# A gated attention unit with a hypermixer: a quarter of each diagonal block turned instead of scored, and transposes by four row tiles

## The chip, the cores and the metric

The kernel runs on one core of a Trainium2 chip. A core has five engines, each with its own instruction stream: TensorE (PE in the profile, with its weight loads PEld beside it), VectorE (DVE), ScalarE (ACT), GpSimd (POOL) and SyncE (SP), which here only issues DMAs. The metric is device time in microseconds, as the median of several runs; less is better. The profile is of one execution, so a span in it stands a little apart from the median of the runs.

## The reference

Eight batches of S = 3200 rows; `u` and `v` have 256 columns, `z` has 64, and the hidden width of the second part is 64.

```python
def _attn_ref(u, v, z):
    scale = 1.0 / S
    scores = scale * np.matmul(z, z.transpose(0, 2, 1))
    attn = np.maximum(scores, 0.0) ** 2
    out = np.matmul(attn, v)
    return (u * out).astype(np.float32)

def _moe_ref(x, w_q, w_k, w_out):
    wq = x @ w_q
    wk = x @ w_k
    scale = 1.0 / np.sqrt(d_hyper)
    W_tok = scale * np.einsum('bsd,btd->bst', wq, wk)
    mixed = np.einsum('bst,btd->bsd', W_tok, x)
    return (np.maximum(mixed, 0.0) @ w_out).astype(np.float32)

def reference(u, v, z, moe_w_q, moe_w_k, moe_w_out):
    return _moe_ref(_attn_ref(u, v, z), moe_w_q, moe_w_k, moe_w_out)
```

`scores` is symmetric, and so is `attn`: a block above the diagonal is the transpose of the one below it.

## The kernel before

The 3200 rows of a batch are 25 row tiles of 128. The columns of `attn` are taken in seven groups: 0 to 5 of 512 columns (four row tiles each) and group 6 (`LASTG`) of the last 128. A group's result needs every row tile's block of `attn` for the group's columns, as weights of a product with `v` that adds up in two PSUM banks.

Such a block comes in one of two ways. It is scored: `scores` multiplies z with z (line 307), `first_stage` takes relu and a scale (DVE at 321 or ACT at 319), `second_stage` squares into a 16-bit buffer `at` (POOL at 332 or ACT at 330). Or it is turned: where `is_turned` says so, the block was scored for an earlier group, and a DMA transpose (line 351, SP's queue) brings its mirror image into a `tt` buffer, or a `ts` buffer for group 6. `tiles` lists in order what is scored: (batch, group, row tile). Two entries make a pair, which shares one PSUM tile of 2 x 512 columns, because z has 64 columns and TensorE's rows hold two of them side by side. `at` has `NAT` = 11 buffers, each for one pair, and a transpose is issued per pair, with 8 blocks of 128 x 128 when both rows go to the same place.

The loop `while groups` runs in phases k. A phase scores three pairs (two when a mixing product "m" takes a place), takes their relu, squares the three pairs of the phase before, and does the second product (`second_product`, emitted at line 369) for row tiles scored at least `LAG` = 2 phases earlier, or turned (`left`). Each phase's TensorE instructions stand in a fixed order: the upper and the lower 64 rows of the array are two lanes (`Streams`, `first_pass`, `second_pass`), each of which does half of the contraction. A row tile of a wide group has four blocks, each done in two halves of 64 rows: eight matmuls 64x256. Extra products go into phases by `mix_due`, `key_due` and the table `chosen`: keys and heads "k", mixing "m", projections "p". When a group is complete, `gate` multiplies by `u` (ACT 506, DVE 507, POOL 509; for group 6 of all but the last batch ACT 499, DVE 500, POOL 501 and 502). `turn_x` and `turn_keys` issue further transposes.

The next batch's data come during the current one, at phases counted from the batch's start: `load_piece` loads pieces of v and z and casts them a few phases later (line 151, POOL on even phases, ACT on odd ones; the tables `V_FIRST` for batch 1 and `V_LATER` for the others give load phase and delay), `turn_z` transposes z, and `spread_z` copies it on ACT (184, 188), to have it in both halves of the partitions.

The order of instructions on each engine is the program's order (`manual_schedule`), and waits come from the data and the buffers. All DMAs of the loop are issued by SP in order. The diff touches the buffers, the list `tiles`, the three stages, `weights`, the tables and the choice among turned rows.

Of the kernel before, what the change touches and what calls it, by code (L numbers as in the profile page):

```python
# [9 lines left out]
FP16 = mybir.dt.float16  # L10
# [6 lines left out]
def kernel(  # L17
# [45 lines left out]
    pat = ctx.enter_context(tc.tile_pool(name="pat", bufs=NAT))  # L63
# [40 lines left out]
    zd0 = {}  # L104
# [130 lines left out]
    LASTG = NG - 1  # L235
# [18 lines left out]
    for b in range(B):  # L254
        for gi in range(NG):
            near = [t for t in range(NT) if is_turned(gi, group_of(t))]
            own = [
                t for t in range(NT) if t not in near and not is_turned(group_of(t), gi)
            ]
            if gi == LASTG:  # L260
                own = [t for t in own if group_of(t) not in FOR_SMALL]
            if b == 0 and gi == 0:
                order = [t for n0, nn in ZCH for t in range(n0, n0 + nn)]
                assert sorted(order) == sorted(near + own)
            else:
# [7 lines left out]
                for _, two in at_:  # L273
                    order = order + two
                if rest and len(rest) % 2:
                    order.remove(rest[-1])
                    order.append(rest[-1])
# [18 lines left out]
    def scores(p0, lead=0):  # L296
        pair = tiles[p0 : p0 + 2]
        sc = ps_tile("sc")
        ats = [[], []]
        for h, (b, gi, tis) in enumerate(pair):  # L300
            w = widths[gi]
            half = h * dqk
            for i in range(W // w):
                ti = tis[min(i, len(tis) - 1)]
                ats[h].append((i * w, h, w, b, ti, starts[gi], half))
        for at, h, w, b, ti, gs, half in sorted(ats[0] + ats[1], key=lambda x: (x[0], x[1] ^ lead)):
            nc.tensor.matmul(  # L307
                out=sc[:, h, at : at + w],
                lhsT=zT[b][half : half + dqk, ds(z_at(b, h) + ti * P, P)],
                rhs=zT[b][half : half + dqk, ds(z_at(b, h) + gs, w)],  # L310
                start=True,
                stop=True,
            )
        return sc

    def first_stage(p0, sc, on_act):
# [6 lines left out]
            )  # L323
        return g

    def second_stage(p0, g, on_act):
        at = pat.tile([P, 2 * W], FP16, tag="at", name="at")
        out = at[:].rearrange("p (a w) -> p a w", a=2)
        if on_act:
            nc.scalar.square(out=out, in_=g[:])  # L330
        else:
            nc.gpsimd.tensor_mul(out=out, in0=g[:], in1=g[:])  # L332
        blocks, turns = [], []
        for h, (b, gi, tis) in enumerate(tiles[p0 : p0 + 2]):
            for i, ti in enumerate(tis):
                made[b, gi, ti] = (at, h * W + i * widths[gi])
            gj = group_of(tis[0])
            if is_turned(gi, gj) or (gj == LASTG and gi in FOR_SMALL):
                blocks.append((b, gi, gj, tis[0] - starts[gj] // P, 1, h * W, (h + 1) * W))
        if len(blocks) == 2 and blocks[0][:3] == blocks[1][:3] and blocks[1][3] == blocks[0][3] + 1:  # L340
            blocks = [blocks[0][:4] + (2, blocks[0][5], blocks[1][6])]
        for b, gi, gj, n0, nn, c0, c1 in blocks:
            if gj == LASTG:
                turned[b, gi, gj] = ptt.tile([P, 1, 4, P], FP16, tag=f"ts{gi}", name=f"ts{gi}")
            elif (b, gi, gj) not in turned:
                home = tt_of[b, gi, gj]
                turned[b, gi, gj] = ptt.tile([P, 4, 4, P], FP16, tag=f"tt{home}", name=f"tt{home}")
            out = turned[b, gi, gj][:].rearrange("p n j t -> p (n j) t")
            turns.append(
                lambda out=out[:, 4 * n0 : 4 * (n0 + nn), :], c0=c0, c1=c1:  # L350
                nc.sync.dma_start_transpose(out=out, in_=at[:, c0:c1])
            )
        return turns

    accs = {}

# [509 lines left out]
    def group_begun(k, b, gi):  # L866
# [5 lines left out]
        if gi == 0 and b + 1 < B:  # L872
# [155 lines left out]
    while groups:  # L1028
# [325 lines left out]
```

## Time and profile before

| | |
|---|---|
| median of 3 runs | 765.5 us (765.41 to 766.83) |
| profiled execution, span | 763.7 us |
| TensorE busy | 754.3 us, 99% |
| weight loads | 618.0 us, 81% |
| ScalarE busy | 551.1 us, 72% |
| GpSimd busy | 537.1 us, 70% |
| VectorE busy | 461.9 us, 60% |
| DMA queue q1, share of 16 engines | 91.2% |
| mean granted TensorE clock | 0.998 |

The span is the time from the first to the last instruction of the profiled execution. In rows of the profile, a line number such as L369 stands for the program's line, `out<-in` for the buffers, and `xN` for the number of instructions in a group. "Idle before" is the time for which an engine had nothing to do ahead of such an instruction, with what released it. TensorE overlaps its matmuls, so the duration of one is longer than the step from one to the next.

### The profile page before, as it was taken

How to read it: one execution, taken by the hardware profiler on the slowest of the kernel's cores; microseconds unless marked ns; L12 is line 12 of the kernel's file. 1: busy time of each engine (PE TensorE's matmuls, PEld its weight loads, DVE VectorE, ACT ScalarE, POOL GpSimd, SP SyncE). 2: the span in 40 equal slices, each digit the busy share in tenths (PEclk: the TensorE clock that was granted, in tenths of full speed). 3: DMA queues.
4: the chain of work that ended last, by engine and by line, in shares of the span. 5: the costliest groups of instructions: out<-in, count | busy, mean ns of one | idle time of the engine just before them, and what ended most of it. 6: DMA issues, size and time to landing. Idle time of an engine off the chain costs nothing.

```text
span 763.7 us, 29059 instructions
## 1 busy us (share of the span) xinstructions
PE 754.3 (99%) x12888; PEld 618.0 (81%) x12888; DVE 461.9 (60%) x458; ACT 551.1 (72%) x651; POOL 537.1 (70%) x351
## 2 busy tenths in 40 slices
PE   9999999999999999999999999999999999999996
PEld 6777888888888887888888888888878888888884
DVE  7655676546755567555665557656566565755534
ACT  8666776677767777687776877759777697776555
POOL 7897797768766678676787668866688665854540
PEclk9999999999999999999999999999999999999999
DMA  8999789887999969997899998999899999798636
GB/s 178 189 197 219 187 187 192 174 181 160 206 196 233 219 166 185 221 235 195 214 177 219 243 195 181 158 228 265 135 223 189 228 250 156 161 222 193 176 74 262
DMA packets 289614, 150.23 MB, mean 197 GB/s; under 512 B 265168, under 2 KB 268752, under 8 KB 289488
## 3 DMA queue, kind: packets, MB, share of 16 engines
q1 hardware_dynamic: 288768, 146.48, 91.2%
q0 software_dynamic: 576, 1.64, 1.1%
q8 instruction: 100, 1.64, 0.9%
q14 instruction: 26, 0.21, 0.1%
q10 hardware_dynamic: 144, 0.26, 0.1%
HBM read 59.38 MB, written 26.21 MB: 112 GB/s over the span
## 4 chain that ended last, share of the span: by engine, by line
PE 97%; DVE 2%; issue 0%; DMA 0%; ACT 0%; DVEq 0%; ACTq 0%
PE acc L369 72%; PE sc L307 12%; PE fo L369 5%; PE qk L369 5%; PE mx L657 1%; DVE x_sb L507 1%; DVE fo L1312 0%; DVE g L321 0%; PE ztp L130 0%; DMA z<-in_z_dram 0%; PE qk L610 0%; DVE zT L136 0%; PE xtx L634 0%; PE hd L644 0%; ACT fo L1316 0%
## 5 line engine op out<-in xcount | busy, mean ns | idle before, releaser
L321 DVE TENSOR_SCALAR g<-sc 128x1024 f32<-128x1024 f32 x329 | 400.5, 1223 | 240.5 <-PE sc L307 225.9
L332 POOL TENSOR_TENSOR at<-g 128x1024 f16<-128x1024 f32 x229 | 431.4, 1893 | 131.1 <-DVE g L321 106.5
L369 PE MATMUL acc<-v_sb,at 64*128 64x256 f16 (+1 forms) x7187 | 461.8, 269 | 1.6 <-DVE x_sb L507 0.5
L369 PEld LDWEIGHTS <-at 64*128 64x128 f16 (+1 forms) x7187 | 353.9, 94 | 86.9 <-PE acc L369 25.4
L330 ACT ACTIVATE at<-g 128x1024 f16<-128x1024 f32 x227 | 236.1, 1056 | 14.3 <-DVE g L321 7.2
L369 PE MATMUL acc<-v_sb,tt 64*128 64x256 f16 x2552 | 178.7, 269 | 0.0
L307 PE MATMUL sc<-zT 64*128 64x512 f16 (+1 forms) x1008 | 165.3, 357 | 0.2
L319 ACT ACTIVATE g<-sc 128x1024 f32<-128x1024 f32 x127 | 130.0, 1024 | 45.5 <-PE sc L307 43.2
L369 PEld LDWEIGHTS <-tt 64*128 64x128 f16 x2552 | 130.1, 94 | 14.2
L509 POOL TENSOR_TENSOR x_sb<-gt,u_sb 128x512 f16<-128x512 f32 x48 | 61.2, 1276 | 66.2 <-ACT gt L506 61.8
L678 ACT ACTIVATE rt<-mx 128x1024 f16<-128x1024 f32 x47 | 47.9, 1024 | 32.6 <-PE mx L657 32.5
L506 ACT COPY gt<-acc 128x512 f32<-128x512 f32 x48 | 28.0, 584 | 46.5 <-PE acc L369 44.7
L307 PEld LDWEIGHTS <-zT 64*128 64x128 f16 x1008 | 51.9, 94 | 8.8 <-issue 1.7
L369 PE MATMUL fo<-wo,rt 64*128 64x256 f16 (+1 forms) x696 | 57.9, 270 | 0.0
L544 ACT CAST qk<-qk 128x512 f16<-128x512 f32 x47 | 27.5, 585 | 34.3 <-PE qk L369 31.6
L369 PEld LDWEIGHTS <-rt 64*128 64x128 f16 (+1 forms) x696 | 35.5, 94 | 15.3 <-PE fo L369 6.3
L507 DVE TENSOR_TENSOR x_sb<-acc,u_sb 128x512 f16<-128x512 f32 x48 | 33.2, 691 | 20.3 <-PE acc L369 19.5
L739 ACT ACTIVATE fo<-fo 128x1024 f32<-128x1024 f32 x39 | 39.9, 1024 | 1.9 <-PE fo L369 1.7
L369 PEld LDWEIGHTS <-x_sb 64*128 64x128 f16 x672 | 29.8, 95 | 4.5 <-PE qk L369 0.9
L369 PE MATMUL qk<-kx,x_sb 64*128 64x64 f16 x672 | 32.8, 190 | 0.0
L369 PE MATMUL qk<-xT_sb,wkq 64*128 64x512 f16 (+3 forms) x118 | 25.8, 326 | 0.0
L369 PE MATMUL qk<-xT_sb,wqk 64*128 64x384 f16 (+3 forms) x148 | 24.8, 296 | 0.0
(86 smaller groups left out, 275.2 us busy)
## 6 DMA issues: line engine op xcount, KB each, us to landing
u_sb<-in_u_dram SPq DMA_DIRECT2D x48, 512.0 KB, 5.5
out_dram<-fo SPq DMA_DIRECT2D x43, 512.0 KB, 4.1
piece<-in_v_dram SPq DMA_DIRECT2D x42, 512.0 KB, 5.2
piece<-in_z_dram SPq DMA_DIRECT2D x7, 512.0 KB, 5.2
tt<-at SPq DMA_TRANSPOSE x162, 4.6
out_dram<-fo SPq DMA_DIRECT2D x9, 256.0 KB, 2.9
piece<-in_z_dram SPq DMA_DIRECT2D x7, 288.0 KB, 4.9
u_sb<-in_u_dram SPq DMA_DIRECT2D x8, 128.0 KB, 4.2
```

Of the source, the lines that this page charges most:

```text
L307: nc.tensor.matmul(out=sc[:, h, at : at + w], lhsT=zT[b][half : half + dqk, ds(z_at(b, h) + ti * P, P)], rhs=zT[b][half : half + dqk, ds(z ...
L319: nc.scalar.activation(out=g[:], in_=sc[:], func=RELU, scale=GSCALE)
L321: nc.vector.tensor_scalar(out=g[:], in0=sc[:], scalar1=0.0, scalar2=GSCALE, op0=AOP.max, op1=AOP.mult)
L330: nc.scalar.square(out=out, in_=g[:])
L332: nc.gpsimd.tensor_mul(out=out, in0=g[:], in1=g[:])
L369: return nc.tensor.matmul(out=self.out, lhsT=self.lhsT(rows), rhs=self.rhs(rows), start=start, stop=stop)
L506: nc.scalar.copy(out=upper[:], in_=accs[1][:])
L507: nc.vector.tensor_mul(out=x[:, 0:n], in0=accs[0][:, 0:n], in1=ug[:, 0:n])
L509: nc.gpsimd.tensor_mul(out=x[:, n : 2 * n], in0=upper[:], in1=ug[:, n : 2 * n])
L544: nc.scalar.copy(out=qks[b, gi][:, 0:gw], in_=out)
L678: nc.scalar.activation(out=out, in_=ps[:], func=RELU)
L739: nc.scalar.mul(out=flat_out[:, sl], in_=part, mul=FINAL_SCALE)
```

## The change

In groups 0 to 5, except group 0 of the first batch and group 5 of the last, the diagonal block (the group's own four row tiles by its 512 columns) is no longer scored whole. Its row tiles 0 and 1 are scored for all 512 columns. Row tiles 2 and 3 are scored for the last 256 columns only, both in one entry of `tiles` (a "half"). Their first 256 columns are the mirror image of the last 256 columns of row tiles 0 and 1, and come by a DMA transpose of four blocks into a new buffer `tc` (the "corner"). The square of the pair that holds row tiles 0 and 1 writes its columns in another order, so that the corner's source lies in one piece.

Row tiles to be turned stand in fours instead of twos, a double buffer holds two pairs (`NAT` = 5 doubles of 4 x 512 columns), and one transpose of up to 16 blocks is issued after the second pair's square. Blocks for group 6 and corners are turned after their own pair. Among turned rows (`left`) those come last whose transposes have not all been issued.

The table of extra products is new, `heading_more` is empty, loads of v for batches 2 and later move by a phase, and `spread_z` for these batches by three. The tables of batch 1 (`V_FIRST`, offset 14) are as before.

```diff
-    NAT = 11
+    NAT = 5
...
-            zd0[c] = pat.tile([P, nn, 2, dqk], FP16, tag="at", name="zd")
+            if c % 2 == 0:
+                zd0["both"] = pat.tile([P, 2, 8, 2, dqk], FP16, tag="at", name="zd")
+            zd0[c] = zd0["both"][:, c % 2, 0:nn, :, :]
...
-    V_LATER = [(7, 5), (9, 4), (11, 4), (13, 3), (14, 3), (15, 3), (17, 4)]
+    V_LATER = [(6, 5), (8, 4), (10, 4), (12, 3), (13, 3), (14, 3), (16, 3)]
...
+    def has_corner(b, gi):
+        return gi < LASTG and (b, gi) not in ((0, 0), (B - 1, LASTG - 1))
+
+    def is_half(gi, tis):
+        return gi < LASTG and len(tis) == 2
...
-                odd = len(tiles) % 2
+                odd = -len(tiles) % 4
+                half = []
+                if has_corner(b, gi):
+                    mine = rows_of(gi)
+                    half = mine[2:]
+                    others = [t for t in own if t not in mine]
+                    own = others[: odd % 2] + mine[:2] + others[odd % 2 :]
                 order, rest = own[:odd], own[odd:]
-                n_, m_ = len(near) // 2, (len(rest) + 1) // 2
+                n_, m_ = len(near) // 4, (len(rest) + 3) // 4
                 at_ = sorted(
-                    [((i + 0.5) / max(n_, 1), near[2 * i : 2 * i + 2]) for i in range(n_)]
-                    + [((i + 0.7) / max(m_, 1), rest[2 * i : 2 * i + 2]) for i in range(m_)]
+                    [((i + 0.5) / max(n_, 1), near[4 * i : 4 * i + 4]) for i in range(n_)]
+                    + [((i + 0.7) / max(m_, 1), rest[4 * i : 4 * i + 4]) for i in range(m_)]
                 )
...
+            if has_corner(b, gi):
+                tiles.append((b, gi, half))
...
-            w = widths[gi]
+            w = W // 2 if is_half(gi, tis) else widths[gi]
+            gs = starts[gi] + (W // 2 if is_half(gi, tis) else 0)
...
+    doubles, corners = {}, {}
+
     def second_stage(p0, g, on_act):
-        at = pat.tile([P, 2 * W], FP16, tag="at", name="at")
-        out = at[:].rearrange("p (a w) -> p a w", a=2)
+        first = p0 // 4 not in doubles
+        if first:
+            doubles[p0 // 4] = pat.tile([P, 4 * W], FP16, tag="at", name="at"), []
+        at, parts = doubles[p0 // 4]
+        here = 2 * W * (p0 // 2 % 2)
+        b, gi, tis = tiles[p0]
+        corner = None
+        if has_corner(b, gi) and tis == rows_of(gi)[:1]:
+            assert tiles[p0 + 1] == (b, gi, rows_of(gi)[1:2])
+            corner = corners[b, gi] = ptt.tile([P, 2, 2, P], FP16, tag="tc", name="tc", bufs=2)
+            out = at[:, here : here + 2 * W].rearrange("p (c a w) -> p a c w", a=2, c=2)
+            in_ = g[:].rearrange("p a (c w) -> p a c w", c=2)
+        else:
+            out = at[:, here : here + 2 * W].rearrange("p (a w) -> p a w", a=2)
+            in_ = g[:]
         if on_act:
-            nc.scalar.square(out=out, in_=g[:])
-        else:
-            nc.gpsimd.tensor_mul(out=out, in0=g[:], in1=g[:])
+            nc.scalar.square(out=out, in_=in_)
+        else:
+            nc.gpsimd.tensor_mul(out=out, in0=in_, in1=in_)
...
+        if corner is not None:
+            turns.append(
+                lambda: nc.sync.dma_start_transpose(
+                    out=corner[:].rearrange("p n j t -> p (n j) t"), in_=at[:, here + W : here + 2 * W]
+                )
+            )
+        if first and p0 // 4 < (NTILE - 1) // 4:
+            now_, parts[:] = [x for x in parts if x[2] == LASTG], [x for x in parts if x[2] != LASTG]
+            parts = now_
+        else:
+            parts.sort(key=lambda x: x[5])
+        for part in parts:
+            was = blocks[-1] if blocks else None
+            if was and was[:3] == part[:3] and was[3] + was[4] == part[3] and was[6] == part[5]:
+                was[4] += 1
+                was[6] = part[6]
+            else:
+                blocks.append(part)
...
+    def turn_blocks(out, in_, key, tis):
+        for ti in tis:
+            turned_by[key + (ti,)] = now[0]
+        nc.sync.dma_start_transpose(out=out, in_=in_)
...
+        if (b, gi) in corners and j < 2 and ti in rows_of(gi)[2:]:
+            return corners[b, gi][rows, j, ti - rows_of(gi)[2], :]
         if (b, gi, ti) in made:
-            at, at0 = made[b, gi, ti]
-            return at[rows, ds(at0 + j * P, P)]
+            at, at0, half_step = made[b, gi, ti]
+            return at[rows, ds(at0 + j % 2 * P + j // 2 * (half_step), P)]
...
-                    k + (14 if b == 0 else 13) + i,
+                    k + (14 if b == 0 else 10) + i,
                     lambda half=half, n0=n0, n1=n1: spread_z(b + 1, half, n0, n1),
...
-    heading_more = {165: -1}
+    heading_more = {}
     chosen = {
-        18: "k", 19: "p", 20: "p", 21: "m", 35: "k", 36: "p", 38: "p", 101: "p", 142: "mp",
-        147: "k", 148: "m", 149: "m", 159: "mp", 161: "p", 163: "m"
+        147: "m", 148: "mp", 149: "k", 150: "mp", 151: "p", 152: "mp", 153: "k", 154: "m",
+        155: "mp", 156: "k", 157: "p",
     }
...
+        if not closes:
+            left.sort(key=lambda t: not all((b, group_of(t), n) in turned_by for n in rows_of(gi)))
```

More of the change, by code (lines that the diff above doesn't have):

```diff
@@ L265 @@
             else:
-                odd = len(tiles) % 2
+                odd = -len(tiles) % 4
[5 more added lines that the diff above has]
+                    own = others[: odd % 2] + mine[:2] + others[odd % 2 :]
                 order, rest = own[:odd], own[odd:]
-                n_, m_ = len(near) // 2, (len(rest) + 1) // 2
+                n_, m_ = len(near) // 4, (len(rest) + 3) // 4
                 at_ = sorted(
-                    [((i + 0.5) / max(n_, 1), near[2 * i : 2 * i + 2]) for i in range(n_)]
-                    + [((i + 0.7) / max(m_, 1), rest[2 * i : 2 * i + 2]) for i in range(m_)]
-                )
[L273 to L277, printed above, removed]
+                    [((i + 0.5) / max(n_, 1), near[4 * i : 4 * i + 4]) for i in range(n_)]
+                    + [((i + 0.7) / max(m_, 1), rest[4 * i : 4 * i + 4]) for i in range(m_)]
+                )
+                for _, four in at_:
+                    order = order + four
+                short = rest[len(rest) // 4 * 4 :]
+                for t in short:
+                    order.remove(t)
+                order += short
             many = W // widths[gi]
             tiles += [(b, gi, order[i : i + many]) for i in range(0, len(order), many)]
+            if has_corner(b, gi):
+                tiles.append((b, gi, half))
             ends[b, gi] = len(tiles)
@@ L304, in scores @@
                 ti = tis[min(i, len(tis) - 1)]
-                ats[h].append((i * w, h, w, b, ti, starts[gi], half))
+                ats[h].append((i * w, h, w, b, ti, gs, half))
         for at, h, w, b, ti, gs, half in sorted(ats[0] + ats[1], key=lambda x: (x[0], x[1] ^ lead)):
@@ L329, in second_stage @@
         if on_act:
-            nc.scalar.square(out=out, in_=g[:])
+            nc.scalar.square(out=out, in_=in_)
         else:
-            nc.gpsimd.tensor_mul(out=out, in0=g[:], in1=g[:])
-        blocks, turns = [], []
+            nc.gpsimd.tensor_mul(out=out, in0=in_, in1=in_)
         for h, (b, gi, tis) in enumerate(tiles[p0 : p0 + 2]):
             for i, ti in enumerate(tis):
-                made[b, gi, ti] = (at, h * W + i * widths[gi])
+                at0 = here + h * W + i * widths[gi]
+                half_step = 2 * P
+                if is_half(gi, tis):
+                    at0 = here + h * W + (i - 1) * W // 2
+                elif corner is not None:
+                    at0 = here + h * W // 2
+                    half_step = W
+                made[b, gi, ti] = at, at0, half_step
@@ L337, in second_stage @@
             gj = group_of(tis[0])
             if is_turned(gi, gj) or (gj == LASTG and gi in FOR_SMALL):
-                blocks.append((b, gi, gj, tis[0] - starts[gj] // P, 1, h * W, (h + 1) * W))
-        if len(blocks) == 2 and blocks[0][:3] == blocks[1][:3] and blocks[1][3] == blocks[0][3] + 1:
-            blocks = [blocks[0][:4] + (2, blocks[0][5], blocks[1][6])]
+                n0, c0 = tis[0] - starts[gj] // P, here + h * W
+                parts.append([b, gi, gj, n0, 1, c0, c0 + W])
@@ new lines, in second_stage @@
+        blocks, turns = [], []
+        if corner is not None:
[9 more added lines that the diff above has]
+            parts.sort(key=lambda x: x[5])
```

6 lines of the change are left out of this document (4 added, 2 removed).

## The prediction

> **What bounds the kernel now.** I read the busy line and the clock line of the page first, then the engines by stretch, then the chain of waits by line. Columns of the stretches: length, then PE, PEld, DVE, ACT and POOL busy with their counts, granted clock, DMA share, GB/s.
>
> ```profile
> span 763.7 us, 29059 instructions
> ...
> PE 754.3 (99%) x12888; PEld 618.0 (81%) x12888; DVE 461.9 (60%) x458; ACT 551.1 (72%) x651; POOL 537.1 (70%) x351
> ```
> ```profile
> 9.00:740.00 731.00, 729.37 (x12692) 600.42 (x12691) 448.72 (x437) 534.22 (x628) 531.22 (x337) 1.00 0.95 196
> 740.00:763.70 23.70, 17.07 (x139) 12.45 (x137) 9.69 (x14) 10.93 (x17) 1.27 (x1) 0.95 0.62 222
> ```
> ```profile
> by line: PE acc L369 72.1%; PE sc L307 12.5%; PE fo L369 5.0%; PE qk L369 4.6%; PE mx L657 1.5%; DVE x_sb L507 0.7%; DVE fo L1312 0.4%; issue 0.4%; DVE g L321 0.3%; PE ztp L130 0.3%; DMA z<-in_z_dram 0.3%; PE qk L610 0.2%; DVE zT L136 0.2%;
> ```
>
> From 9 to 740 us TensorE is busy in 729.37 of 731.00 us at full clock. Every other engine has spare time, and the chain is TensorE all the way. So two things only move the time: TensorE work taken away, and new holes in it. The opening and the last 23.7 us keep their order in the change, and I price them at nothing: what hides there is work that does not differ, and if the last phases shift it is by parts of a microsecond. The span is 763.7 and the three runs have a median of 765.5, so I add 1.8 to any span.
>
> **What is removed: 23 pairs of scores.** In 46 groups (0 to 5 of eight batches, without the very first and the very last) row tiles 2 and 3 are scored on 256 columns instead of 512. Counting the instructions of the changed program, full-width score matmuls go from 880 to 788 and 92 of 256 columns are new. In columns that is 92 x 256, or 46 full matmuls: 23 pairs of row tiles out of 456. The second product keeps its number of blocks; only the source of some weights changes.
>
> ```profile
> 304.53 0.38 PE L307 MATMUL sc<-zT 64*128 64x512 f16 x2
> ...
> 305.21 1.91 PE L369 MATMUL acc<-v_sb,at 64*128 64x256 f16 x32
> ...
> 309.38 0.59 PE L307 MATMUL sc<-zT 64*128 64x512 f16 x4
> ...
> 309.81 1.04 PE L369 MATMUL acc<-v_sb,at 64*128 64x256 f16 x16
> ```
>
> The duration of one matmul is latency, since they overlap; what counts is the step. Four score matmuls (two pairs) last 0.59 us, two last 0.38, so a pair costs 0.21. The chain agrees: 12.5% of 763.7 is 95.5 us, and 880/2 = 440 full pairs with the 16 narrow ones of group 6 make 456, 0.209 each. 23 x 0.21 = 4.8 us. Against it: two matmuls of 256 take the place of one of 512 in the halves. The second product has that width: (1.91 - 1.04)/16 = 0.054 each, so two cost 0.109 where half a pair costs 0.105; 46 x 0.004 is 0.2 us at most, and I take 0.1. Net -4.7.
>
> **What lies beside it.** The 23 pairs also save relu and square work.
>
> ```profile
> L321 DVE TENSOR_SCALAR g<-sc 128x1024 f32<-128x1024 f32 x329 | 400.5, 1223 | 240.5 <-PE sc L307 225.9
> L332 POOL TENSOR_TENSOR at<-g 128x1024 f16<-128x1024 f32 x229 | 431.4, 1893 | 131.1 <-DVE g L321 106.5
> ```
>
> The relu falls from 329 to 314 on DVE (15 x 1.223 = 18 us) and the squares from 229 to 206 on POOL (23 x 1.893 = 44 us). DVE waits 225.9 us for scores, so that is not on the path and I price it at nothing; were TensorE not busy for 99%, it would matter. The 46 corner squares write in another order; no row shows that form, but at twice the time 26 on POOL would add 26 x 1.9 = 49 us, about what it saves, again beside TensorE. From below, a strided square that costs no more leaves the saving whole.
>
> **What is moved: two waits at the first change of batch.** Fewer phases per batch bring the next batch forward, and I looked for operands that come late by following each wait of the changed program to its producer. I found two places where TensorE gets there first, both between batch 0 and batch 1, where the spreading of z and the loading of v keep their old offsets.
>
> The first: row tile 12 of batch 1 is now scored in the phase that opens group 5 of batch 0, one phase earlier. In that phase ScalarE still makes the last copy of the spread z, behind the copy that gates the previous group. The same place in the trace of before:
>
> ```profile
> 77.11 0.38 PE L307 MATMUL sc<-zT 64*128 64x512 f16 x2
> ...
> 77.36 0.58 ACT L506 COPY gt<-acc 128x512 f32<-128x512 f32 x1 [3.13 <-PE acc L369]
> ...
> 77.97 0.94 ACT L188 COPY zT<-zT 64x896 f16<-64x896 f16 x1
> ```
> ```profile
> 732.07 0.39 PE L307 MATMUL sc<-zT 64*128 64x128 f16 x8
> ```
>
> The phase begins at 77.11, the copy ends at 78.91, 1.8 us later. Before that score stand only eight narrow score matmuls, at most 0.39 us. TensorE waits some 1.5 us. Queued behind it are all matmuls of the phase, since their order is fixed. If more work stood before the score the wait would fall towards 0; if ScalarE had one relu more in front it would be 1.0 more.
>
> The second: rows 20 to 23 of v for batch 1 are cast on POOL in the second phase of that batch's group 0, and the new order puts row 20 into that same phase. Before, these rows were read a phase or two later. The first phase of the group in the trace of before:
>
> ```profile
> 94.43 0.40 PE L307 MATMUL sc<-zT 64*128 64x512 f16 x2
> ...
> 94.69 0.42 DVE L500 COPY gt<-acc 128x256 f32<-128x256 f32 x1 [0.78 <-PE acc L369]
> ...
> 96.59 0.73 POOL L501 TENSOR_TENSOR gt<-gt 128x256 f32<-128x256 f32 x1
> ...
> 97.39 0.73 POOL L502 TENSOR_TENSOR xl<-gt,u_sb 128x256 f16<-128x256 f32 x1
> ...
> 98.06 1.04 POOL L151 CAST v_sb<-piece 128x1024 f16<-128x1024 f32 x1
> ...
> 99.06 1.90 POOL L332 TENSOR_TENSOR at<-g 128x1024 f16<-128x1024 f32 x1
> ```
>
> In the changed order POOL has to add and multiply for the gate, square twice, and then cast. Counted from the start of that phase: the gate's operands come after 0.7 (94.43 to 95.11, the end of the DVE copy), then 0.8 + 0.8 + 1.9 + 1.9 + 1.04, together 7.1 us. TensorE's first phase there holds seven row tiles and three pairs, 7 x 8 x 0.054 + 3 x 0.21 = 3.7, and row 20 is fourth in the next, behind one pair and 16 matmuls, 1.1 more: it arrives at 4.8. The wait is 2.3; with one more pair in front, 2.1. I take 2.2, between 0 (POOL does the cast before a square) and 4.4 (POOL begins as late as in the trace, 96.59, that is 2.2 after the phase). In later batches both steps come earlier in the changed table, and I found no such wait.
>
> **What is added: turning by fours.** Two pairs share a buffer, there are five such doubles in place of eleven singles, and one transpose of 16 blocks replaces two of eight. 46 corner transposes are new.
>
> ```profile
> L351 SPq DMA_TRANSPOSE tt<-at x162: 1195/1373/4432, 13.1 to 719.6; - x162
> ...
>   ACT at L330: 4.8, 2
> ...
> DMA to landing us min/median/max: 2.5/4.6/9.7
> ```
> ```profile
> q1 hardware_dynamic: 288768, 146.48, 91.2%
> ```
>
> SP's issues on this line go from 186 to 152, 34 x 1.37 = 47 us less of its queue if an issue of 16 blocks costs no more than one of eight, none less if it costs double. The blocks turned grow by 46 x 4 = 184; at the queue's 0.912 x 763.7/288768 = 2.4 ns of span per packet and 128 packets per block, 184 x 128 x 2.4 ns = 57 us of a queue that runs at 91%. That would take the queue to 98% if a packet's time stays what it was. If part of that time is packets standing in line behind others, which no row separates, it is less. Either way landings can grow, not shrink. TensorE does not read what a transpose brings until two phases later or more, and a corner three to five. So what becomes late first is the buffer: a square waits until the transposes out of its buffer have landed. From a transpose's square to the square that takes the buffer again there are now nine pairs, three phases of six row tiles, 3 x (6 x 8 x 0.054 + 3 x 0.21) = 9.7 us, where eleven pairs gave 11.9. A square (1.9), an issue (1.4) and a landing (4.6) take 7.9; the slowest landing of 9.7 takes 13. In the trace two squares waited so, 4.8 us in total, and TensorE had no hole there. I take 0.4 us: at least 0, and at most 6, reasoned in the second rival.
>
> The sum: 763.7 - 4.7 + 1.5 + 2.2 + 0.4 = 763.1, and with 1.8 a time of 764.9.
>
> The Trainium skill, "TensorE: Matmul & The Clock Gate", Part 1, says that TensorE's clock falls to half after an idle window of some 3.4 us. Neither of my two waits reaches that alone, and the trace of before has a mean clock of 0.95 only in the last stretch, which agrees in direction. By that rule a wait of 3.4 us or more would cost about half the time to the next raise on top, an estimate of 1.7 us from the page's window: 766.6 by the page and 764.9 by the rows.
>
> **The rivals.** First, the waits do not bite: POOL and ScalarE run ahead of the places that I compared, or the scheduler's order within the phase leaves more work in front. Then 763.7 - 4.7 + 0.4 is 759.4, with 1.8 a time of 761.2. For it speaks that TensorE waited for no engine but DVE in the whole run before; against it, that the operands are named by the program and the durations are fixed.
>
> Second, slower: the buffers. If a landing takes 2 us longer with 16 blocks, then 9.9 us are needed where 9.7 are there, and squares slip in the tightest stretches. The second product reads a square about two phases after the scoring; half of that is slack. With about 30 reuses in such stretches, and TensorE held for 0.2 us in each, 6 us are lost in place of 0.4: 770.5. It decides from the point where median landing passes 6.4 us (9.7 - 1.9 - 1.4). For it: 91.2%, and 4.8 us waited already. Against: fewer issues on SP's queue.
>
> Third, slower as well: the clock. In the last stretch TensorE is idle for 6.6 us and the granted clock is lower by 0.05 over 23.7 us, 1.2 us. If each of my two waits does the same, 2 x 1.2 = 2.4 are added: 767.3.
>
> Fourth, the change does not save what it says, because a half pair holds a TensorE slot as long as a full one. Then the 4.7 vanish: 764.9 + 4.7 = 769.6. Against it: eight score matmuls of 128 columns last 0.39, four of 512 last 0.59, so a narrower one is cheaper.
>
> **How the numbers follow.** My own sum has 0.54, the free waits 0.20, the buffers 0.16, the clock 0.06, the missing saving 0.04. A measurement of this kernel can tell about 0.2%, 1.5 us: faster is below 764.0, slower above 767.0. My sum's own range, with the two waits between 1.5 and 5.4 together in place of 3.7, is 762.7 to 766.6; it falls a third on faster and the rest on the same. So faster is 0.20 + 0.18 = 0.38, same 0.34 + 0.05 from milder buffers = 0.39, slower 0.23. The range for 8 in 10 reaches from the free waits to mild buffer trouble: 760.8 to 768.8. The time is 764.9.
>
> **What would show it.** Right: 23 pairs fewer at the score line and its share of the chain near 12%; at about 75 us a hole in TensorE released by the ScalarE copy, about 1.5 us, and at some 90 us one released by the POOL cast, about 2.2; TensorE otherwise above 99% busy; squares waiting for DMA no more than some 20 us and mostly without a hole behind them. Wrong: holes in TensorE released by squares, spread over all batches (then the buffers), or no hole at the change of batch at all (then 761).

## The result

The changed kernel took 817.27 us (median of 4 runs, 810.72 to 819.4) against 765.88 us before: a ratio of 1.066, with a 95% interval of 1.0626 to 1.0694. The profiled execution has a span of 816.8 us. The prediction was 764.9 us with a range of 760.8 to 768.8, so it missed by 52 us and on the wrong side.

Lines of the page of the changed kernel, in the order of those shown of before: span, busy times, the DMA queue.

```profile
span 816.8 us, 28929 instructions
...
PE 768.2 (94%) x12864; PEld 632.2 (77%) x12864; DVE 443.4 (54%) x443; ACT 542.8 (66%) x640; POOL 496.3 (61%) x331
...
q1 hardware_dynamic: 311232, 152.50, 89.2%
```

TensorE is idle for 816.8 - 768.2 = 48.6 us, where it was 9.4: 39 us of holes. And it is busy for 14 us more with fewer columns to score, so its work became slower as well. The DMA queue's share did not rise. The waits of the changed kernel by engine (engine and line, what it waited for, us in total, times, longest) say what released the holes:

```profile
PE acc L434 <- DMA tc<-at: 22.0, 9, 4.1
PE qk L677 <- DVE hT L665: 4.9, 3, 1.8
PE sc L325 <- ACT fo L806: 2.2, 2, 2.0
PE acc L434 <- POOL v_sb L153: 1.8, 1, 1.8
...
PE sc L325 <- ACT zT L190: 1.4, 1, 1.4
```
```profile
ACT at L363 <- DMA tt<-at: 53.3, 22, 6.0
...
ACT at L363 <- DMA tc<-at: 14.2, 5, 3.8
```
```profile
POOL at L365 <- DMA tt<-at: 66.4, 29, 4.9
POOL at L365 <- DMA tc<-at: 31.1, 11, 5.3
```

Nine times TensorE waits for a corner, up to 4.1 us. The squares on both engines wait for transposes out of their buffers for 165 us together; before, it was 4.8 us. The two waits that the prediction named are there too (`v_sb` from POOL, `zT` from ScalarE).

The nine waits have a place: seven stand in the closing phase of group 4, one in each of batches 0 to 6. The one of batch 4 in the timelines of SP, ScalarE and TensorE (start, length, what; in brackets the idle time before it and its releaser; the corner's square is the first of the two shown of ScalarE, by the program's order on that engine):

```profile
445.91 5.01 SPq L418 DMA_TRANSPOSE tt<-at  x1
451.01 1.20 SPq L618 DMA_TRANSPOSE kx<-qk  x1
452.31 1.25 SPq L585 DMA_TRANSPOSE xT_sb<-x_sb  x1
453.62 2.35 SPq L418 DMA_TRANSPOSE ts<-at  x1
456.06 0.53 SPq L807 DMA_DIRECT2D out_dram<-fo  x1
456.70 3.24 SPq L418 DMA_TRANSPOSE tt<-at  x1
460.03 0.53 SPq L149 DMA_DIRECT2D piece<-in_v_dram  x1
460.61 0.44 SPq L197 DMA_DIRECT2D u_sb<-in_u_dram  x1
461.14 1.27 SPq L383 DMA_TRANSPOSE tc<-at  x1
```
```profile
446.37 1.06 ACT L363 ACTIVATE at<-g 128x1024 f16<-128x1024 f32 x1
...
452.98 1.06 ACT L363 ACTIVATE at<-g 128x1024 f16<-128x1024 f32 x1 [3.66 <-DMA tt<-at]
```
```profile
463.91 0.71 PE L434 MATMUL acc<-v_sb,at 64*128 64x256 f16 x9
467.23 0.28 PE L434 MATMUL acc<-v_sb,tc 64*128 64x256 f16 x1 [2.62 <-DMA tc<-at]
...
467.59 3.67 PE L434 MATMUL acc<-v_sb,tt 64*128 64x256 f16 x32
...
472.20 1.91 PE L434 MATMUL acc<-v_sb,tt 64*128 64x256 f16 x32
```

The square that holds the corner's source has no wait and ends at 447.4. Its transpose is issued at 461.14, 13.7 us later: the eight other issues shown stand in front of it on SP, and from 445.91 on they take 14.6 us together. It lands at about 467.2. TensorE came for it at 464.6. In the seven batches the issue stands 10.8 to 15.5 us behind its square, and TensorE comes 12 to 17 us behind it. The later square at 452.98 shows the other side of the same queue: it waits 3.66 us until the `tt` that was issued at 445.91 has landed out of its buffer.

The last two rows show the second loss: 32 matmuls of one form take 3.67 us right after the hole and 1.91 some us later. The stretches of 5 us behind a hole of 2.6 us, behind one of 1.96 us and behind one of 1.8 us, with the granted clock as the third number from the end:

```profile
467.20:472.20 5.00, 4.97 (x58) 3.59 (x60) 0.62 (x1) 1.06 (x1) 1.89 (x1) 0.66 0.88 205
...
747.00:752.00 5.00, 5.00 (x59) 4.18 (x60) 1.44 (x2) 3.21 (x4) 3.12 (x2) 0.66 1.05 250
```
```profile
652.30:657.30 5.00, 5.00 (x83) 4.00 (x85) 2.89 (x3) 4.64 (x7) 1.73 (x1) 1.00 0.82 174
```

A mean of 0.66 over 5 us is half speed for 3.4 us, or 1.7 us lost, behind each hole of 1.96 us and longer; there are eight of those, seven of them the waits for a corner in group 4. That is 14 us of the 51. The Trainium skill, "TensorE: Matmul & The Clock Gate", Part 1, gives half rate and a window of about 3.4 us; the trace agrees with both, but here a hole of 1.96 us was enough; the same hole in e6 left the clock at 1.00 (below).

### The profile page after: what moved, and what is told of

Its sections match the earlier page's. It is cut to its first block, busy times and chain, and to the rows that moved or that the text cites. A ratio compares the mean times of both kernels' runs of the same rounds, so it can differ in the third digit from the quotient of the medians.

```text
span 816.8 us, 28929 instructions
## 1 busy us (share of the span) xinstructions
PE 768.2 (94%) x12864; PEld 632.2 (77%) x12864; DVE 443.4 (54%) x443; ACT 542.8 (66%) x640; POOL 496.3 (61%) x331
## 4 chain that ended last, share of the span: by engine, by line
PE 65%; DMA 17%; ACT 6%; POOL 4%; issue 3%; DVE 2%; SPq 2%; ACTq 0%; POOLq 0%; DVEq 0%
PE acc L434 49%; DMA tt<-at 9%; PE sc L325 8%; DMA tc<-at 4%; PE fo L434 3%; PE qk L434 3%; DMA piece<-in_v_dram 2%; POOL at L365 2%; ACT at L363 2%; ACT g L337 1%; DVE g L339 1%; PE mx L724 1%; SPq L418 1%; POOL v_sb L153 1%; DVE x_sb L574 1%
## 5 line engine op out<-in xcount | busy, mean ns | idle before, releaser
L339 DVE TENSOR_SCALAR g<-sc 128x1024 f32<-128x1024 f32 x314 | 382.4, 1223 | 289.6 <-PE sc L325 278.6
L365 POOL TENSOR_TENSOR at<-g 128x1024 f16<-128x1024 f32 x206 | 388.0, 1893 | 196.9 <-DVE g L339 71.4
L434 PE MATMUL acc<-v_sb,at 64*128 64x256 f16 (+1 forms) x6811 | 464.6, 270 | 7.2 <-POOL v_sb L153 1.8
L434 PE MATMUL acc<-v_sb,tt 64*128 64x256 f16 x2544 | 184.7, 279 | 0.0
L325 PE MATMUL sc<-zT 64*128 64x512 f16 (+2 forms) x1008 | 161.6, 350 | 4.5 <-ACT fo L806 2.2
L434 PEld LDWEIGHTS <-tt 64*128 64x128 f16 x2544 | 137.2, 97 | 16.7 <-issue 0.5
L337 ACT ACTIVATE g<-sc 128x1024 f32<-128x1024 f32 x119 | 121.7, 1022 | 27.1 <-PE sc L325 26.4
L434 PE MATMUL acc<-v_sb,tc 64*128 64x256 f16 x368 | 56.0, 271 | 22.0 <-DMA tc<-at 22.0
L325 PEld LDWEIGHTS <-zT 64*128 64x128 f16 x1008 | 56.3, 95 | 15.1 <-issue 5.7
L434 PEld LDWEIGHTS <-tc 64*128 64x128 f16 x368 | 33.3, 94 | 28.1 <-DMA tc<-at 24.7
L434 PEld LDWEIGHTS <-rt 64*128 64x128 f16 (+1 forms) x688 | 37.3, 95 | 11.9 <-PE fo L434 2.8
```

Source lines behind the costliest of these rows:

```text
L325: nc.tensor.matmul(out=sc[:, h, at : at + w], lhsT=zT[b][half : half + dqk, ds(z_at(b, h) + ti * P, P)], rhs=zT[b][half : half + dqk, ds(z ...
L337: nc.scalar.activation(out=g[:], in_=sc[:], func=RELU, scale=GSCALE)
L339: nc.vector.tensor_scalar(out=g[:], in0=sc[:], scalar1=0.0, scalar2=GSCALE, op0=AOP.max, op1=AOP.mult)
L365: nc.gpsimd.tensor_mul(out=out, in0=in_, in1=in_)
L434: return nc.tensor.matmul(out=self.out, lhsT=self.lhsT(rows), rhs=self.rhs(rows), start=start, stop=stop)
```

## The experiments

The theory after the first look was that the doubles are at fault: a transpose waits for its second pair, comes as 16 blocks, and holds a coarse buffer. Rivals: the 8% more blocks overfill the DMA queue; or the corner is read too soon.

**e1: a buffer and a transpose for each pair again.**

```diff
-    NAT = 5
+    NAT = 10
...
-        at, parts = doubles[p0 // 4]
-        here = 2 * W * (p0 // 2 % 2)
+        at, parts = pat.tile([P, 2 * W], FP16, tag="at", name="at"), []
+        here = 0
```

> The changed kernel with its corners, its order and its tables, but each pair has a buffer of its own again (ten singles) and its own transposes of up to 8 blocks. Theory 'doubles' (a transpose that waits for the second pair and then lands late as 16 blocks, out of five coarse buffers, makes squares and corners late): the 50 us go, 762 to 770 us. Rival 'blocks' (the 8% more turned blocks overfill the DMA queue, in whatever form they are issued): 800 us or more. Rival 'corner order' (a corner is read too soon by the order of the row tiles, in group 4 above all): most of the loss stays, 790 us or more.

814.22 us, ratio 1.0637 (1.0551 to 1.0724). TensorE waits as before for corners:

```profile
PE acc L425 <- DMA tc<-at: 26.1, 11, 4.8
```

The theory of the doubles falls: without them some 3 us of 51 go, and that lies within the spread of the runs.

**e2: no corners, doubles kept.**

```diff
     def has_corner(b, gi):
-        return gi < LASTG and (b, gi) not in ((0, 0), (B - 1, LASTG - 1))
+        return False
```

> The changed kernel without corners: every diagonal block is scored whole, as before, and the table of extra products is that of before, since there are again as many phases; the doubles and the transposes by four stay. Theory 'doubles': still slow, 795 us or more. Rival 'blocks' and rival 'corner order': the loss goes, 764 to 772 us.

771.02 us, 1.0074 (1.0052 to 1.0097): the corners carry the loss. The rest of the change (fours, doubles, the order and the load times) costs some 5 us without any corner.

**e3: ten buffers in the kernel before. e4: ten buffers and 48 idle transposes.**

```diff
-    NAT = 11
+    NAT = 10
```
```diff
+        b_, gi_, tis_ = tiles[p0]
+        if gi_ < LASTG and any(t[1] == gi_ and t[2][0] == rows_of(gi_)[1] for t in tiles[p0 : p0 + 2]):
+            corner = ptt.tile([P, 4, P], FP16, tag="tc", name="tc", bufs=2)
+            turns.append(lambda: nc.sync.dma_start_transpose(out=corner[:], in_=at[:, W : 2 * W]))
```

> The kernel before with ten single buffers for the squares in place of eleven, nothing else. If the mere number of buffers that the change leaves (five doubles hold ten pairs) were the cause: 790 us or more. Theory 'doubles' (their coarse grain, not their number) and rival 'blocks': 765 to 769 us.

> The kernel before with ten single buffers, and beside it 48 transposes of four blocks more, one for each of groups 0 to 5 at the place of a corner, into a tile that nobody reads. Rival 'blocks': 795 us or more, since the DMA queue has the load of the change. Theory 'doubles' and rival 'corner order': within 4 us of the run with ten buffers alone.

e3: 765.66 us, 1.0003 (0.9986 to 1.002). One buffer fewer costs nothing. e4: 776.57 us, 1.0146 (1.0063 to 1.0229), between the two expectations: transposes that nobody reads cost some 11 us (5 to 18 by the interval), but not 51. The load is a part, and the wait for the corner has to be another.

**e5: corners turned but not read. e6: nor turned.** (The last line of e5's edit stands in a conditional whose other branch never holds; that is left out here. e6 has e5's edit as well.)

```diff
         if (b, gi) in corners and j < 2 and ti in rows_of(gi)[2:]:
-            return corners[b, gi][rows, j, ti - rows_of(gi)[2], :]
+            at, at0, half_step = made[b, gi, ti]
+            return at[rows, ds(at0 + W // 2 + j * P, P)]
```
```diff
-        if corner is not None:
+        if corner is not None and False:
             turns.append(
```

> The changed kernel with all its corner transposes issued, but nobody reads them: where a corner would be the weights, the second product takes the row tile's own last 256 columns again, so a quarter of each diagonal block is wrong. Theory 'late corner' (TensorE waits for the landing of a corner, and everything behind it slips): 763 to 778 us, with no wait of TensorE for a turned block. Rival 'load' (the 8% more blocks fill the queue, and the squares wait for buffers): 795 us or more.

> The run with unread corners, and their 46 transposes are not issued either: the saved scoring alone, without load and without wait. Both theories: 762 to 768 us. Its distance to the run with unread corners is the price of the load alone: under 'late corner' 3 to 12 us (the 48 unread transposes cost the kernel before 11), under 'load' 30 us or more.

e5: 791.21 us, 1.0329 (1.0278 to 1.038). e6: 774.03 us, 1.0105 (1.0075 to 1.0134). So 817 - 791 = 26 us are TensorE's waits for corners with what follows from them, 791 - 774 = 17 us are the mere presence of 46 more transposes, and 774 - 766 = 8 us are lost with neither, though 23 pairs of scores are saved. e5 lies between the two expectations, and so do the 17 us of load; both theories had e6 too low.

The saving itself: e6 has TensorE busy for 751.64 us, where before it was 754.3.

```profile
0.00:771.70 771.70, 751.64 (x12864) 622.19 (x12864) 443.54 (x443) 543.29 (x640) 496.45 (x331) 1.00 0.91 195
```

That is 2.6 less at full clock, of 4.7 that were forecast. A matmul 64x256 lasts 0.27 us where the step is 0.054, so each added hole may bring some 0.2 us of latency into the busy time again, and the true saving is probably not smaller; this was not separated. TensorE is idle for 20.1 us, 10.7 more than before, and that less the 2.6 is the loss of 8.

**e7: halves read last. e8: no corner in group 4.**

```diff
         consumed += new
+        if has_corner(b, gi):
+            rows_.sort(key=lambda t: t in rows_of(gi)[2:])
```
```diff
-        return gi < LASTG and (b, gi) not in ((0, 0), (B - 1, LASTG - 1))
+        return gi < LASTG and gi != 4 and (b, gi) not in ((0, 0), (B - 1, LASTG - 1))
```

> The changed kernel, with the row tiles of a half read last in their phase, some 2 us later than now in the closing phase of group 4. Theory 'late corner': about 2 us less in each of seven batches and a little in group 3, 795 to 805 us. Rival 'load': 812 us or more.

> The changed kernel without a corner in group 4, whose diagonal block is scored whole (8 half pairs, 0.8 us of scoring). Theory 'late corner', with the waits in the closing phase of group 4: 34 us go, 778 to 790 us. Rival 'load': 8 of 46 transposes fewer, 805 us or more.

e7: 801.73 us, 1.0466 (1.0436 to 1.0497). A reader that comes some 2 us later takes 15.5 us off, and the direct waits fall from 22.0 to this:

```profile
PE acc L434 <- DMA tc<-at: 7.4, 5, 4.0
```

The late corner is shown. e8: 805.0 us, 1.0509 (1.0478 to 1.054), only 12 us less where 34 were expected, and at the lower end of what the rival 'load' had. TensorE's direct waits for corners fall to 7.7 us in e8, and its longest row says where the rest went:

```profile
PE qk L677 <- DVE hT L665: 12.0, 4, 4.1
```

`hT` stands for the heads: they need a cast on ScalarE (`qk`), and ScalarE's squares stand in front of that, waiting for buffers. One such place in e8:

```profile
449.61 1.06 ACT L363 ACTIVATE at<-g 128x1024 f16<-128x1024 f32 x1 [3.26 <-DMA tt<-at]
...
451.47 0.58 ACT L611 CAST qk<-qk 128x512 f16<-128x512 f32 x1
```

The corner of group 4 was only the first to show that SP's transposes are late at that place; taken away, the next reader waits. The clock takes no less for it: its mean is 0.979 in e8's profiled execution and 0.983 in the changed kernel's.

**e9: the loads for batch 1 a phase earlier, on e6. e10: singles, on e6.**

```diff
-    V_FIRST = [(13, 3), (14, 3), (15, 3), (16, 3), (17, 3), (18, 3), (19, 3)]
+    V_FIRST = [(12, 3), (13, 3), (14, 3), (15, 3), (16, 3), (17, 3), (18, 3)]
...
-                    k + (14 if b == 0 else 10) + i,
+                    k + (13 if b == 0 else 10) + i,
```

> The run with neither corner transposes nor their readers (774.0 us), with the loads of v for batch 1 and the spreading of its z one phase earlier. The two waits that the prediction named stand in that run's trace with 1.9 and 2.0 us. If they are what they seem: 770 to 771 us. Rival: they only move to another place, 773 us or more.

> The run with neither corner transposes nor their readers (774.0 us), with ten single buffers and transposes by pair in place of doubles. It takes the rest of the loss apart, some 9 us beside the two waits. Theory 'doubles cost the rest': 765 to 769 us. Rival 'the new order and table cost it': 773 to 775 us.

e6 has the two waits at their places, with the lengths that the changed kernel shows. The 1.9 and 2.0 us of the expectation are the longest of two other rows, `hT` and `fo`:

```profile
PE qk L678 <- DVE hT L666: 3.2, 2, 1.9
PE sc L325 <- ACT fo L807: 2.2, 2, 2.0
PE acc L434 <- POOL v_sb L153: 1.8, 1, 1.8
PE sc L325 <- ACT zT L190: 1.4, 1, 1.4
```

These four rows are 8.6 of the 10.7 us by which TensorE is idle for longer than before. In e9 the last two are gone from TensorE's waits, and yet it took 773.07 us, 1.0091 (1.0062 to 1.0121). The rival had that: in their place TensorE waits 1.7 us for squares of POOL, which e6 does not show.

```profile
PE acc L434 <- POOL at L365: 1.7, 2, 1.0
```

And the clock took 1.7 us in e9's profiled execution. Both runs have a hole of 1.96 us ahead of a score that waits for ScalarE's `fo` copy; the 5 us behind it in e9, and then in e6:

```profile
701.50:706.50 5.00, 5.00 (x59) 4.19 (x60) 1.66 (x2) 3.19 (x4) 3.12 (x2) 0.66 1.09 258
```
```profile
703.20:708.20 5.00, 4.99 (x87) 4.47 (x88) 2.45 (x2) 3.22 (x4) 3.13 (x2) 1.00 1.09 258
```

Why the same hole had it in one run and not in the other was not shown.

e10: 771.91 us, 1.0076 (1.0047 to 1.0105), between its two expectations: the doubles cost 2 of the 8 us. What is left belongs to the new order and tables. Beside the two named waits, the largest wait of e10 is one of a score for a PSUM bank that ScalarE's projection copy holds; why it comes late was not looked into.

```profile
PE sc L323 <- ACT fo L798: 2.3, 3, 2.0
```

**e11, e13, e14: the idle transposes by size and number.** e11 turns one block in place of four, e13 two transposes of one block, e14 one of eight (into one buffer in place of two).

```diff
-            corner = ptt.tile([P, 4, P], FP16, tag="tc", name="tc", bufs=2)
+            corner = ptt.tile([P, 1, P], FP16, tag="tc", name="tc", bufs=2)
```

> The kernel before with ten buffers and 48 transposes that nobody reads, of one block each in place of four (four blocks: 776.6 us). Theory 'bytes' (the blocks fill the DMA queue): a quarter of the 11 us, 767 to 770 us. Rival 'issue' (each transpose takes its time on SP's queue, whatever its size): 774 to 778 us.

> The kernel before with ten buffers and 96 transposes of one block that nobody reads, two at each of 48 places. 48 of one block and 48 of four cost about the same (776.3 and 776.6 us), and each took some 1.3 us of SP's queue. Theory 'issue': twice as many issues, 785 us or more. Rival 'bytes': 96 blocks are half of 48 x 4, 768 to 773 us.

> The kernel before with ten buffers and 48 transposes of eight blocks that nobody reads. Theory 'issue': a little above 48 of four blocks, since an issue of eight takes 1.7 in place of 1.4 us, 776 to 784 us. Rival 'bytes': twice 48 x 4, 786 us or more.

| beside ten buffers | blocks added | time, us | ratio (interval) | SP's issuing, sum, us | issue of a `tt` after its phase began, median, us |
|---|---|---|---|---|---|
| nothing (e3) | 0 | 765.66 | 1.0003 (0.9986 to 1.002) | 608 | 6.5 |
| 48 of one block (e11) | 48 | 776.29 | 1.0133 (1.0006 to 1.0261) | 671 | 7.5 |
| 48 of four (e4) | 192 | 776.57 | 1.0146 (1.0063 to 1.0229) | 683 | 8.2 |
| 48 of eight (e14) | 384 | 799.29 | 1.0442 (1.0396 to 1.0488) | 704 | 9.2 |
| 96 of one (e13) | 96 | 819.55 | 1.0722 (1.0677 to 1.0767) | 736 | 10.9 |

The last two columns are worked out from the traces: the lengths of SP's DMA issues added up, and for each `tt` the time from the first matmul of the phase that issues it. From the end of its square to its issue a `tt` waits for a median of 4.9, 6.1, 6.5, 7.5 and 8.7 us in the five runs. e11 and e13 went the way of 'issue', e14 the way of 'bytes'. So neither holds alone: 96 blocks in 96 transposes cost more than 384 in 48, and e14 above e4 says that blocks are not free. There the squares wait 25 us for the idle transposes themselves, in e4 7.6. The times of the five runs rise with SP's issuing and with the lateness of a `tt`. The landing of the `tt` does not change. Their line in e3 and in e13:

```profile
L351 SPq DMA_TRANSPOSE tt<-at x162: 1198/1398/4422, 13.1 to 719.6; - x162
...
  ACT at L330: 8.8, 6
  POOL at L332: 8.6, 7
...
DMA to landing us min/median/max: 2.4/4.7/8.0
```
```profile
L357 SPq DMA_TRANSPOSE tt<-at x162: 1217/1344/3366, 13.0 to 776.2; - x162
...
  ACT at L330: 85.1, 32
  POOL at L332: 81.7, 32
...
DMA to landing us min/median/max: 2.4/4.7/7.7
```

The median landing stays at 4.7 us from the issue, but the squares' waits grow from 17 to 167 us. In e13 a `tt` is late because it is issued late, not because it moves slowly. And the loss is steep: the first 48 cost some 11 us (0.5 to 20 by the interval), the next 48 another 43.

**e12: corners in groups 0 and 5 only, with singles.**

```diff
-        return gi < LASTG and (b, gi) not in ((0, 0), (B - 1, LASTG - 1))
+        return gi in (0, 5) and (b, gi) not in ((0, 0), (B - 1, LASTG - 1))
```

> The changed kernel with corners in groups 0 and 5 only, singles instead of doubles. Those stand where the DMA queue has room or the reader comes late. If late corners and load bite in groups 1 to 4 alone: 764 to 771 us, the two waits at the change of batch included. Rival 'load anywhere costs the same': 14 corners of 46, 775 us or more.

775.15 us, 1.0118 (1.0088 to 1.0149), just outside the first expectation and on the rival's edge. TensorE's waits hold none for a corner. It took 3 us more than e10 (771.91, no transposes), but it scores 32 diagonal blocks whole that e10 does not, and TensorE is busy for 754.7 us in its trace against 750.6 in e10's. So 14 corners at these places cost nothing that the two runs show.

**e15 to e18: fewer issues on SP.** e15 has the loads of u issued by GpSimd and the stores by ScalarE; e16 adds the mends of e7 and e9. e17 and e18 move only the stores, on e4 and on the changed kernel with those two mends.

```diff
-        nc.sync.dma_start(out=us[b, gi][:, 0:nn, :], in_=rows(u, b)[:, n0 : n0 + nn, :])
+        nc.gpsimd.dma_start(out=us[b, gi][:, 0:nn, :], in_=rows(u, b)[:, n0 : n0 + nn, :])
...
-            b, gi, src, [(False, nc.sync, widths[gi] // P)]
+            b, gi, src, [(False, nc.scalar, widths[gi] // P)]
```

> The changed kernel, computing what it should, with the loads of u issued by GpSimd and the stores of the loop by ScalarE behind its own copy, in place of SP. The same bytes move; SP has some 64 us less to issue and no longer waits for ScalarE's copies there. Theory 'issue' (SP's queue runs late, so corners land late and squares wait for buffers): 775 to 800 us. Rival 'bytes': 810 us or more.

> The run before this one, with the halves read last in their phase and the loads for batch 1 one phase earlier as well. Theory 'issue': most of the late corners go, 765 to 780 us; below 764 only if the new table costs nothing. Rival 'bytes': 790 us or more.

> The run with 48 unread transposes of four blocks (776.6 us), with the loop's stores issued by ScalarE behind its own copies in place of SP. Only some 29 us of issues and SP's waits for those copies go; the loads of u, which slowed the transposes' landings in e15 when GpSimd issued them, stay on SP. Theory 'issue': 767 to 773 us. Rival 'bytes or landing': 775 us or more.

> The changed kernel with the stores issued by ScalarE, the halves read last and the loads for batch 1 a phase earlier; the loads of u stay on SP. e7 had 801.7 us with the halves last alone. Theory 'issue': 780 to 796 us. Rival 'bytes or landing': 798 us or more.

e15: 818.01 us, 1.0689 (1.0629 to 1.0748). e16: 808.3 us, 1.0546 (1.0516 to 1.0576). e17: 784.82 us, 1.0267 (1.0208 to 1.0325). e18: 808.8 us, 1.0564 (1.0546 to 1.0581). All four went the rival's way; none gained by it. The traces show two things. The landings grew: in e15 the `tt` of up to 16 blocks take a median of 7.4 us against 6.2 in the changed kernel, and in e18, where the loads of u stay on SP, 7.0; so it was not shown that the loads of u slow them. And SP does not come much sooner: in e17 the sum of its issues falls from 683 to 666 us, while a `tt` is still issued 7.8 us after its phase began (8.2 in e4), and SP waits longer for ScalarE's squares. e4's row and e17's:

```profile
SPq L355 <- ACT at L330: 42.1, 32, 2.9
```
```profile
SPq L355 <- ACT at L330: 54.6, 36, 6.3
```

So SP's time for issues alone is not what sets the price. There is a rival that was not tested: in e17 ScalarE spends 16 us on the 46 stores that it now issues, and in e15 GpSimd 33 us on its loads, and both engines make the squares. The account that fits the waits, argued and not shown, is a loop: SP issues in order and waits for a square, the square waits for a landing out of its buffer, and that landing had to be issued by SP. More transposes, and larger ones, were shown to lengthen it (e11, e4, e14, e13). That less work on SP for anything else would shorten it was not shown. None of the versions tried beats the kernel before.

## Why the prediction was wrong

**What bounds the kernel** was right for the kernel before, and it was used too simply: "Every other engine has spare time" does not hold for a queue that issues in order and for buffers that come back through it. SP's issues add up to 615 of 764 us in the kernel before, and the prediction did not look at that.

**The two waits at the change of batch** were right in place, cause and size: 1.4 and 1.8 us against 1.5 and 2.2. **The saving** of 4.7 us shows as 2.6 in e6's busy time and 3.7 in e10's.

**The step that failed first** is the sentence that TensorE does not read what a transpose brings until two phases later or more, and a corner three to five, so that the buffer becomes late first. The count of phases was right: group 4's corner is read three phases after its square. But group 4 has the fewest scored row tiles of groups 0 to 5 (13 of 25) and is done in two phases, so TensorE came 12 to 17 us after the square, and the corner's issue alone stood 10.8 to 15.5 us behind it, with its landing still to come. The term stood at nothing and measured 26 us (e5). Some 7 of them are the clock's: half speed lasts 27 us in the changed kernel's trace and 14 us in e5's, the last phases left out.

**The second** is the loop's time: 7.9 us for square, issue and landing against 9.7 between two uses. The working left out how long a ready transpose stands in SP's queue. That could be had from the trace of before: there a `tt` is issued a median of 4.95 us after the end of its square. The working also counted the issue twice, since the landing of 4.6 us is counted from the issue's start. Put right, the estimate is 1.9 + 4.95 + 4.6 = 11.5 us: within the 11.9 that eleven buffers gave, and above the 9.7 that the change leaves. (e3, with ten single buffers, still cost nothing: a late square is not yet a hole of TensorE.) The price of 0.4 us, at most 6, measured 17 for the corners' transposes (e5 against e6), and some 5 for the fours and their order without corners (e2; partly the same as the rest below). Of the two cases that the prediction had for SP's queue, "47 us less" if an issue of 16 blocks costs no more than one of eight and "none less" if it costs double, even the second was too good: such a `tt` takes a median of 3.34 us against 1.37, so 82 of them take the 283 us that 162 took (281), and 46 corners add 68. The lines of the changed kernel:

```profile
L418 SPq DMA_TRANSPOSE tt<-at x82: 1419/3344/5640, 14.1 to 760.2; - x82
```
```profile
L383 SPq DMA_TRANSPOSE tc<-at x46: 1188/1220/2517, 24.6 to 758.3; - x46
```

**The rivals.** The first, that the waits do not bite, falls: both stand in the trace. The second, the buffers, had the mechanism and the side, at 0.16 and 770.5 us. Its condition was wrong: a median landing above 6.4 us. The landing of a `tt` rose to 6.2, and with singles (e1) it is 4.7, while the loss stayed; what grew there is the time from the square to the issue, from 4.95 to 7.15 us. The third, the clock, had the kind of loss, but not its place: behind the two named waits it did not fall, as the 5 us after each in the changed kernel show, and behind eight other holes it took 1.7 us each.

```profile
84.10:89.10 5.00, 4.94 (x88) 4.42 (x90) 2.36 (x2) 3.51 (x4) 3.69 (x4) 1.00 1.06 333
```
```profile
107.90:112.90 5.00, 5.00 (x84) 3.94 (x85) 3.03 (x3) 2.94 (x4) 4.36 (x3) 1.00 1.07 223
```

The fourth falls: TensorE's busy time fell.

**The rest** of the order and the table, priced at nothing, cost some 7 us (e10's 771.9 less the 764.5 that the sum gives without buffers), of which up to 2 may be saving that did not come. Of its waits, `hT` and `fo` stand beside the two named ones in e6; why these operands come late in the new order was not looked into.

## What to carry to other kernels

Before adding a DMA to a queue that issues in order, measure in the trace how long a ready transfer stands in that queue, place by place (here a median of 4.95 us before the change, and up to 15.5 us at the places that mattered after it); its landing time does not tell. Where buffers come back through that queue, an added issue costs little while there is slack and then steeply (11 us for 48, 54 for 96). Price every new hole of TensorE with what the clock takes behind it, and ask of each turned block how late it may be in the group with the fewest row tiles.

## What was not expected of the hardware

Half the granted clock for 3.4 us can follow a hole of 1.9 us, and the length alone does not decide. The stretches of 5 us behind a hole of 1.87 us and behind one of 2.10 us in e13 (columns as above):

```profile
50.00:55.00 5.00, 4.56 (x52) 3.23 (x54) 1.02 (x1) 4.34 (x5) 3.49 (x2) 0.66 0.94 180
647.95:652.95 5.00, 5.00 (x100) 4.51 (x101) 1.71 (x3) 3.31 (x4) 0.85 (x2) 1.00 1.09 290
```

An issue of a transpose on SP takes about 1.2 us for one block as for four (medians 1.19 and 1.23, e11 and e4), 1.40 for eight (e14) and 3.34 for up to sixteen (the changed kernel).
